# Sparse attention and a gated MLP in one kernel: the transfers of weight blocks get sort keys of their own

## The chip, the cores and the metric

The kernel runs on one core of a Trainium2 chip. Its engines work side by side, each through its own list of instructions in order: TensorE (PE) multiplies, VectorE (DVE), ScalarE (ACT) and GpSimd (POOL) do the rest, and SyncE (SP) issues all the transfers from memory. They wait for one another through semaphores. The metric is the device time of one execution in microseconds, the median of several runs.

## The reference

Eight batches of attention with 8 heads, 576 positions and 64 columns per head. The first four heads see a band of 32 positions, the others every 32nd position. Its output is the input of a gated MLP that mixes positions with a 576 x 576 matrix.

```python
scores = scale * np.matmul(q, k.transpose(0, 1, 3, 2))
scores = np.where(masks[None, :, :, :], scores, -1000000000.0)
attn = np.exp(scores - np.max(scores, axis=-1, keepdims=True))
attn = attn / (np.sum(attn, axis=-1, keepdims=True) + 1e-09)
x = np.matmul(attn, v)                    # heads side by side: B, S, 512

h = np.maximum(x @ w_in, 0.0)             # w_in: 512 x 1024
u, v = (h[..., :512], h[..., 512:])
v_n = (v - mu) / np.sqrt(var + 1e-06)     # mean and variance over the 512 columns
v_s = np.einsum('ts,bsd->btd', w_spatial, v_n) + b_spatial[None, :, None]
return ((u * v_s) @ w_out).astype(np.float32)   # w_out: 512 x 512
```

## The kernel before

**Work.** Attention is done for pairs of heads, numbered `t` = 4 b + hp for batch b: two pairs with the band (`local_attention`) and two with the stride (`strided_attention`) in each batch. Scores go into PSUM (L460 and L603), DVE and ACT make the softmax (maximum or mask, exponential L517, sums, L422), DVE transposes the weights in blocks (L541, L657), ACT, POOL and DVE copy the pieces into `ptl` or `pts` (L370, L368), and TensorE multiplies them with the values (L570, L673). The result x^T is split into a rounded part and a remainder (ACT L390, DVE L378), because every large product is done as three products of rounded float32 parts.

The MLP of a batch has these steps: `moe_1` multiplies the v half (L870: 4 tiles of 128 positions, each 4 blocks of 3 matmuls with 512 columns) and normalises it in `chain` (ACT L828, DVE L833 to L841, POOL's power L846, DVE L853), then the u half (L912, 288 columns). `moe_tail` does the 64 last positions of one or two batches. `moe_2` multiplies with the spatial matrix (L993, and L1005 and L1006 for the tail rows), gates with u (DVE L1015), and multiplies with `w_out` (L1035); ACT takes the output out of PSUM (L390).

**Weights.** `weights` brings 12 blocks of 128 rows: of `w_in` the u half and the v half of four row blocks (here u0 to u3 and v0 to v3) and four of `w_out` (o0 to o3). They come as 64-bit numbers of 512 KB a block, and `weight` turns each into two float32 parts: ACT scales the upper words (L746), POOL or DVE takes the low bits (L754, L751), DVE merges (L762), then one engine rounds (L368 on ACT, L370 elsewhere) and DVE subtracts the remainder (L378). The first four blocks in the order of their conversion land in one buffer (`vn_0`), the others in turn in `u` and `g` buffers, so a later one waits until an earlier one is converted. `spatial_weights` brings the four blocks of the spatial matrix (`x_0` and `x_1`, each with two) and its tail (`x_2`).

**Order.** Nothing runs in the order in which it is written. Every operation is added with a key, the engines that can do it, and costs; `Program.order` plays the program through with these costs, lets every engine take the smallest key among the operations that are ready, and the instructions are written out in the order and on the engines that came out. `KEYS` holds numbers that set the order: `a` for the attention of `t` = 0 to 7, `v`, `u`, `o`, `s` and `t` for the weight blocks, `fill` for the clearing of buffers, `lead` for later attention, `dp`, `dpt` and `near` for rules of choice. A transfer is an operation of SP with a key too: for a weight block it was the key of the conversion less 25 (in `weight` and `spatial_weights`). Fillers (L1168) are matmuls that keep TensorE busy at the start. SP's list is a queue as well: a transfer whose buffer isn't free holds up all those behind it.

Of the kernel before, what the change touches and what calls it, by code (L numbers as in the profile page):

```python
# [11 lines left out]
I32 = mybir.dt.int32  # L12
# [25 lines left out]
TAIL = S - 4 * P  # L38
NT = 4
KEYS = {  # L40
    "a": (-1127.3, -1221.6, -672.3, -526.1, 101.7, 33.0, 113.1, 239.5,),
    "v": (-238.9, -1399.6, -76.4, -73.7,),
    "u": (-43.5, -131.3, -12.3, -34.7,),
    "s": (684.8, 251.9, 2902.8, 2024.9,),
    "t": (1654.0,),
    "o": (6.6, -58.9, 103.7, 587.0,),
    "cst": (-1558.0,),
    "lead": (-1.36,),
    "fill": (50.5, 1235.4, -3578.4, 1164.7, -177.7, 809.5,),
    "dp": (849, -9544,),  # L50
    "dpt": (181.75,),
    "near": (198.57,),
}
WARM_END, WARM_GAP, WARM_COST, WARM_COLS, WARM_SHARE = 110000.0, 700.0, 427.0, 256, 0.8
PE_MASKED, APART = (0, 1, 2, 3), (0, 1)
# [254 lines left out]
def attention_moe(ctx, tc, qT, kT, vl, vs, cst, eye, w_in, w_out, wsp, wtail, out):  # L310
# [85 lines left out]
    def load(key, dst, src, writes, nbytes, reads=()):  # L396
        add(key, [(DMA, nbytes / DMA_RATE)], lambda eng: eng.dma_start(dst(), src), reads, writes)
# [323 lines left out]
    def x_tok(t):  # L721
        return [(xs[t], i, c0) for i in range(2) for c0 in ((0, 3) if t % NHP < 2 else (0, 1))]

    def weight(key, src, n, dst, tok, stage):

        buf, i = stage
        if src.dtype == F32:
            val = lambda: buf().bitcast(F32).rearrange(FLAT[len(buf.ring.shape)])[:, 2 * i * n : 2 * i * n + n]
            load(key - 25, val, src, [(buf, i, 0), (buf, i, 1)], P * n * 4)
        else:
            raw = lambda dt: buf().bitcast(F32).rearrange(FLAT[len(buf.ring.shape)])[
                :, 2 * i * n : 2 * (i + 1) * n
            ].bitcast(dt)
            half = lambda j, dt=I32: raw(dt).rearrange("p (n t) -> p n t", t=2)[:, :, j]
            low, top = (buf, i, 0), (buf, i, 1)  # L740
            val = lambda dt=F32: half(1, dt)
            load(key - 25, lambda: raw(I32), src.bitcast(I32), [low, top], P * n * 8)

            add(
                key, [(ACT, 110 + 0.87 * n)],
                lambda eng: eng.activation(val(), val(), AF.Prelu, scale=2.0**-112, alpha=2.0**32),  # L746
                [], [top],
            )
            def lowest(eng):
                if hasattr(eng, "bn_stats"):  # L750
                    eng.tensor_scalar(half(0), half(0), 29, None, op0=ALU.logical_shift_right)  # L751
                else:
                    byte = raw(U8).rearrange("p (n t) -> p n t", t=8)[:, :, 3]
                    eng.tensor_scalar(half(0), byte, 1 / 32, -15.5 / 32, op0=ALU.mult, op1=ALU.add)  # L754
# [5 lines left out]
            add(  # L760
                key, [(DVE, 70 + 1.04 * n)],
                lambda eng: eng.scalar_tensor_tensor(  # L762
                    half(1), half(1), 3, half(0),
                    op0=ALU.logical_shift_left, op1=ALU.bitwise_or,
                ),
                [low], [top], port=(DVE,),
            )
# [26 lines left out]

    def spatial_weights():
        for i in range(NT):
            key = KEYS["s"][i]
# [451 lines left out]
```

## Time and profile before

| | |
|---|---|
| median of 3 runs | 526.38 us (526.30 to 526.54) |
| the profiled execution | 526.95 us, its span 524.8 us, mean clock of TensorE 0.993 |
| start of the last matmuls (L1035) and of ACT's last copy | 515.0 us and 521.5 us |
| VectorE's longest full stretch | 20 to 80 us |
| weight blocks | 12 x 512 KB, and 6 x 288 KB for the spatial matrix |

The span is the time from the first to the last instruction of the profiled execution. A row of the engines' list in order of time gives the start in us, the duration in us, the engine, the line of the code, the operation, what it writes and reads, and how many in a row; in brackets the idle time before it and what ended it. In a group of the page the numbers behind the bar are the busy time in us and the mean of one in ns, then the engine's idle time before them. TensorE's clock is given as a share of its full speed.

### The profile page before, as it was taken

To read this page: it belongs to the slowest core of one execution; us is meant where nothing else is said; L and a number is where in the kernel's file an instruction comes from. 1 tells how busy PE (TensorE), PEld (TensorE's weight loads), DVE (VectorE), ACT (ScalarE), POOL (GpSimd) and SP (SyncE) were. 2 spreads that over 40 slices of the span, in tenths; PEclk is the share of its full clock that TensorE was granted. 3 is DMA by queue.
4 is the path that set the end of the run, shared out by engine and by line. 5 is a ranking of instruction groups with operands and counts; after the bars stand their busy time and mean duration, and the time that the engine had idled before them with its cause. 6 is when DMAs were issued, how large, how long until landed. Compare 5 with 4: busy or idle time off the path is not lost.

```text
span 524.8 us, 14567 instructions
## 1 busy us (share of the span) xinstructions
PE 509.3 (97%) x5982; PEld 467.8 (89%) x5982; DVE 327.1 (62%) x1019; ACT 238.1 (45%) x738; POOL 87.9 (17%) x170
## 2 busy tenths in 40 slices
PE   6798999999999999999999999999999999999997
PEld 3567799888998899989999899998999899998997
DVE  3999998684754848558556767757557652426132
ACT  6677956655653665126532365324543243213111
POOL 2364423120210212002110120102101020001000
PEclk9799999999999999999999999999999999999999
DMA  7779353622233213142222222332021200110011
GB/s 247 263 263 347 133 195 103 188 92 88 66 134 125 87 58 117 55 134 78 79 103 78 85 78 80 132 116 70 3 78 64 87 1 1 46 45 1 1 45 47
DMA packets 26242, 52.65 MB, mean 100 GB/s; under 512 B 3136, under 2 KB 11584, under 8 KB 26176
## 3 DMA queue, kind: packets, MB, share of 16 engines
q1 hardware_dynamic: 26176, 51.72, 30.0%
q8 instruction: 47, 0.77, 0.6%
q14 instruction: 19, 0.16, 0.1%
HBM read 42.27 MB, written 9.44 MB: 99 GB/s over the span
## 4 chain that ended last, share of the span: by engine, by line
PE 85%; DVE 6%; DMA 2%; POOL 2%; issue 2%; ACT 2%; SPq 0%; POOLq 0%; DVEq 0%; ACTq 0%
PE m L1035 20%; PE m L993 17%; PE m L912 17%; PE m L870 17%; PE po L673 3%; PE po L570 3%; PE s L460 2%; PE s L603 2%; PE m L1005 2%; PE m L1006 2%; DMA k<-kT 1%; DMA kbd<-kT 1%; POOL bn L846 1%; POOL ptl L370 1%; DVE bn L833 1%
## 5 line engine op out<-in xcount | busy, mean ns | idle before, releaser
L993 PE MATMUL m<-wsp_sb,vn 128*128 128x288 f32 x768 | 111.5, 296 | 1.0 <-DVE wsp_sb L378 1.0
L1035 PE MATMUL m<-g,w_out_sb 128*128 128x288 f32 x768 | 107.6, 298 | 0.3 <-DVE g L378 0.3
L912 PE MATMUL m<-x,w_in_sb 128*128 128x288 f32 x768 | 105.5, 297 | 1.8 <-ACT vv L828 1.1
L993 PEld LDWEIGHTS m<-wsp_sb,vn 128*128 128x128 f32 x768 | 105.1, 189 | 2.1 <-DVE wsp_sb L378 1.3
L912 PEld LDWEIGHTS m<-x,w_in_sb 128*128 128x128 f32 x768 | 103.3, 188 | 3.4 <-ACT vv L828 1.3
L1035 PEld LDWEIGHTS m<-g,w_out_sb 128*128 128x128 f32 x768 | 103.5, 188 | 1.1 <-DVE g L378 0.5
L870 PE MATMUL m<-w_in_sb,x 128*128 128x512 f32 (+1 forms) x408 | 99.1, 398 | 0.1
L870 PEld LDWEIGHTS m<-w_in_sb,x 128*128 128x128 f32 (+1 forms) x408 | 74.2, 185 | 19.6 <-DVE w_in_sb L378 0.4
L390 ACT COPY o<-m 128x288 f32<-128x288 f32 x60 | 23.7, 399 | 94.8 <-PE m L1035 88.5
L846 POOL TENSOR_TENSOR bn<-bn,sel 128x1 f32<-128x1 f32 (+1 forms) x37 | 22.3, 604 | 201.4 <-DVE bn L841 178.6
L1015 DVE TENSOR_TENSOR u<-m,u 128x288 f32<-128x288 f32 x64 | 28.2, 454 | 41.1 <-PE m L1006 40.7
L370 POOL TENSOR_SCALAR ptl<-pc 32x320 f32<-32x320 f32 (+3 forms) x77 | 30.3, 394 | 125.0 <-DVE pc L541 50.9
L517 ACT ACTIVATE pl<-pl,ml 128x64 f32<-128x64 f32 (+1 forms) x140 | 46.8, 337 | 3.4 <-DVE ml L497 3.4
L828 ACT ACTIVATE vv<-m 128x512 f32<-128x512 f32 (+1 forms) x37 | 22.1, 597 | 48.8 <-PE m L870 47.4
L378 DVE TENSOR_TENSOR x<-po,x 128x288 fp32r<-128x288 f32 x64 | 27.5, 447 | 25.0 <-ACT x L390 24.5
L926 ACT ACTIVATE u<-m 128x288 f32<-128x288 f32 x64 | 25.7, 409 | 36.7 <-PE m L912 36.2
L833 DVE BATCH_NORM_STATS2 bn<-vv 128x6 f32<-128x512 f32 (+1 forms) x37 | 25.5, 689 | 25.0 <-ACT vv L828 24.6
L853 DVE TENSOR_SCALAR vv<-vv,bn 128x512 f32<-128x512 f32 (+1 forms) x37 | 20.5, 556 | 17.1 <-POOL bn L846 17.0
L378 DVE TENSOR_TENSOR g<-u,g 128x288 fp32r<-128x288 f32 x64 | 28.3, 456 | 3.4 <-ACT g L368 2.1
L390 ACT CAST x<-po 128x288 fp32r<-128x288 f32 x53 | 20.4, 399 | 17.2 <-PE po L570 10.5
L392 DVE CAST x<-po 128x288 fp32r<-128x288 f32 x11 | 4.9, 453 | 36.7 <-PE po L673 28.3
L368 ACT COPY ptl<-pc 32x320 f32<-32x320 f32 (+3 forms) x69 | 24.4, 354 | 5.3 <-DVE pc L541 4.0
(118 smaller groups left out, 588.7 us busy)
## 6 DMA issues: line engine op xcount, KB each, us to landing
q<-qT SPq DMA_DIRECT2D x32, 295.0 KB, 4.2
outT<-o SPq DMA_DIRECT2D x64, 144.0 KB, 1.8
v_raw<-vs SPq DMA_DIRECT2D x15, 512.0 KB, 3.6
v_raw<-vl SPq DMA_DIRECT2D x16, 384.0 KB, 4.2
k<-kT SPq DMA_DIRECT2D x16, 304.0 KB, 4.6
kbd<-kT SPq DMA_DIRECT2D x32, 144.0 KB, 3.9
vn<-w_in SPq DMA_DIRECT2D x4, 512.0 KB, 5.5
u<-w_in SPq DMA_DIRECT2D x3, 512.0 KB, 6.5
```

The lines of the kernel that those rows point to most:

```text
L370: eng.tensor_scalar(dst(), src(), 1.0, 0.0, op0=ALU.mult, op1=ALU.add)
L378: eng.tensor_tensor(dst(), src(), f32(hi()), op=ALU.subtract)
L390: eng.copy(dst(), src())
L517: eng.activation(p_sb()[:m, u, :], src, AF.Exp, bias=st()[:m, u : u + 1], scale=SCALE if masked else -1.0, **total,)
L833: lambda eng: eng.bn_stats(bn()[:m, 0:6], v()[:m]), [(v,)], [(bn,)],
L846: lambda eng: eng.tensor_tensor(bn()[:m, 9:10], bn()[:m, 8:9], sel[:m, 0:1], op=ALU.pow),
L870: eng.matmul(v_ps()[:m, :], x_at(kt)[:, a, :], w_in_sb[:, w, kt, HF:], start=(n == 0 and i == 0), stop=(n == NT - 1 and i == 2),)
L912: eng.matmul(u_ps()[:, :HS], w_in_sb[:, w, kt, f * P : (f + 1) * P], xs[NHP * b + kt]()[:, a, r], start=(n == 0 and i == 0), stop=(n == NT ...
L926: lambda eng, u=u, f=f, u_ps=u_ps: eng.activation(u()[:, f * HS : (f + 1) * HS], u_ps()[:, :HS], AF.Relu),
L993: eng.matmul(s_ps()[:, :HS], vn()[:, a, kt, fs], wsp_sb[:, w, kt, r], start=(kt == 0 and i == 0), stop=False,)
L1015: lambda eng, ug=ug, s_ps=s_ps: eng.tensor_tensor(ug(), s_ps()[:, :HS], ug(), op=ALU.mult),
L1035: eng.matmul(o_ps()[:, :HS], w_out_sb[:, w, f, e * P : (e + 1) * P], g[a]()[:, f, :], start=(f == 0 and i == 0), stop=(f == NT - 1 and i = ...
```

## The change

The transfers of all weight blocks get keys of their own (`lv`, `lu`, `lo`, `ls`), where they had the key of the conversion less 25. All other numbers of `KEYS` are new too. The operations are the same; what changes is their order, the choice among engines and which buffer a block lands in. The new file has four lines more, so its line numbers are 4 higher from there on (L766 for L762).

```diff
 KEYS = {
-    "v": (-238.9, -1399.6, -76.4, -73.7,),
-    "u": (-43.5, -131.3, -12.3, -34.7,),
+    "v": (-216.6, -1140.4, -156.0, 19.8,),
+    "u": (-158.4, -165.3, 0.3, 367.0,),
...
+    "lv": (-430.1, -2526.4, -200.5, -140.6,),
+    "lu": (-99.7, -488.1, -137.6, -250.6,),
+    "lo": (435.1, 82.8, -874.1, 81.6,),
+    "ls": (781.6, 39.6, 3113.7, 831.6, 1021.7,),
...
-    def weight(key, src, n, dst, tok, stage):
+    def weight(key, fetch, src, n, dst, tok, stage):
...
-            load(key - 25, val, src, [(buf, i, 0), (buf, i, 1)], P * n * 4)
+            load(fetch, val, src, [(buf, i, 0), (buf, i, 1)], P * n * 4)
...
-            load(key - 25, lambda: raw(I32), src.bitcast(I32), [low, top], P * n * 8)
+            load(fetch, lambda: raw(I32), src.bitcast(I32), [low, top], P * n * 8)
...
                 jobs.append((
-                    KEYS[name][i], w_in[rows, cols], HF,
+                    KEYS[name][i], KEYS["l" + name][i], w_in[rows, cols], HF,
...
-                KEYS["o"][i], w_out[rows, :], DM, lambda j, i=i: w_out_sb[:, j, i], ("w_out", i),
+                KEYS["o"][i], KEYS["lo"][i], w_out[rows, :], DM, lambda j, i=i: w_out_sb[:, j, i], ("w_out", i),
...
-            load(key - 25, src, wsp[i * P : (i + 1) * P, :], [half], P * S * 4)
+            load(KEYS["ls"][i], src, wsp[i * P : (i + 1) * P, :], [half], P * S * 4)
...
-            load(key - 25, lambda i=i: raw(i), wtail[i], [halves[i]], P * S * 4)
+            load(KEYS["ls"][NT], lambda i=i: raw(i), wtail[i], [halves[i]], P * S * 4)
```

**First place: transfers after the start.** SP's queue from the 17th row on, before. `vn_0` holds v2 here, `u_0` v3, `g_0` o1, `u_1` u0, `g_1` u3 and `u_2` u2.

```order
L397 DMA vn_0_93<-w_in 128x1024
L397 DMA u_0_427<-w_in 128x1024
L397 DMA g_0_449<-w_out 128x1024
L397 DMA u_1_477<-w_in 128x1024
L397 DMA g_1_496<-w_in 128x1024
L397 DMA q_4_531<-qT 128x590
L397 DMA k_2_540<-kT 128x608
L397 DMA u_2_551<-w_in 128x1024
```

The same place now. `u_0` is v2, `g_1` v3, `u_1` u2, `vn_0` u0, `u_2` u3, and `x_0` is block 1 of the spatial matrix.

```order
L401 DMA u_0_402<-w_in 128x1024
L401 DMA g_1_428<-w_in 128x1024
L401 DMA u_1_450<-w_in 128x1024
L401 DMA vn_0_93<-w_in 128x1024
L401 DMA q_4_496<-qT 128x590
L401 DMA k_2_511<-kT 128x608
L401 DMA v_raw_3_534<-vl 128x768
L401 DMA u_2_547<-w_in 128x1024
L401 DMA x_0_332<-wsp 128x576
```

The `w_out` block has left this place (it comes six rows later, in `g_0`), u2 has moved ahead of u0, and u3, which stood among the five, now takes the buffer that v2 leaves.

**Second place: conversion on VectorE.** VectorE's rows from about 38 us on, before; between the last row of `x_6` and these stand a merge (of `u_1`) and the remainder of o1.

```order
L762 SCALAR_TENSOR_TENSOR g_1_496<-g_1_496 128x512
L378 TENSOR_TENSOR w_in_sb_62<-u_1_477,w_in_sb_62 128x512
L833 BN_STATS bn_0_578<-vv_0_571 128x6
L378 TENSOR_TENSOR w_in_sb_62<-g_1_496,w_in_sb_62 128x512
L837 BN_AGGR bn_0_578<-bn_0_578 128x2
L833 BN_STATS bn_1_594<-vv_1_582 128x6
L841 TENSOR_SCALAR bn_0_578<-bn_0_578 128x1
L762 SCALAR_TENSOR_TENSOR u_2_551<-u_2_551 128x512
L837 BN_AGGR bn_1_594<-bn_1_594 128x2
L853 TENSOR_SCALAR vv_0_571<-vv_0_571,bn_0_578 128x512
L841 TENSOR_SCALAR bn_1_594<-bn_1_594 128x1
L378 TENSOR_TENSOR w_in_sb_62<-u_2_551,w_in_sb_62 128x512
```

And now; only a merge (L766, of `vn_0`) stands between `x_6` and these.

```order
L382 TENSOR_TENSOR w_in_sb_62<-u_1_450,w_in_sb_62 128x512
L382 TENSOR_TENSOR w_in_sb_62<-vn_0_93,w_in_sb_62 128x512
L837 BN_STATS bn_0_575<-vv_0_568 128x6
L837 BN_STATS bn_1_586<-vv_1_577 128x6
L841 BN_AGGR bn_0_575<-bn_0_575 128x2
L841 BN_AGGR bn_1_586<-bn_1_586 128x2
L845 TENSOR_SCALAR bn_0_575<-bn_0_575 128x1
L845 TENSOR_SCALAR bn_1_586<-bn_1_586 128x1
L766 SCALAR_TENSOR_TENSOR u_2_547<-u_2_547 128x512
L857 TENSOR_SCALAR vv_0_568<-vv_0_568,bn_0_575 128x512
L382 TENSOR_TENSOR wsp_sb_64<-x_0_332,wsp_sb_64 128x576
L382 TENSOR_TENSOR w_in_sb_62<-u_2_547,w_in_sb_62 128x512
```

The last remainder of `w_in` is u2's (`u_2`) before and u3's (`u_2`) now, and a spatial block has come ahead of it. On TensorE the blocks of L912 follow this order: `m_8` and `m_9` take `x_3` and `x_4` and then, past an L460, `x_5` and `x_6` before; now `x_3` to `x_5`, then `x_6`, then the L460.

**Third place: ahead of the first L1035.** VectorE before, at the products with the gate (`u_4`):

```order
L417 RECIPROCAL ml0_78<-ml0_78 128x10
L422 TENSOR_TENSOR pl0_76<-pl0_76,ml0_78 128x640
L378 TENSOR_TENSOR tail_0_996<-vv_4_929,tail_0_996 64x512
L541 STREAM_TRANSPOSE pc_5_1019<-pl0_76 128x640
L378 TENSOR_TENSOR x_7_1028<-po_8_1012,x_7_1028 128x288
L370 TENSOR_SCALAR ptl_73<-pc_5_1019 32x8x32
L378 TENSOR_TENSOR x_7_1028<-po_9_1021,x_7_1028 128x288
L370 TENSOR_SCALAR ptl_73<-pc_5_1019 32x2x32
L1015 TENSOR_TENSOR u_4_712<-m_17_917,u_4_712 128x288
L1015 TENSOR_TENSOR u_4_712<-m_18_933,u_4_712 128x288
L1015 TENSOR_TENSOR u_4_712<-m_19_947,u_4_712 128x288
L1015 TENSOR_TENSOR u_4_712<-m_20_957,u_4_712 128x288
```

And now (the two masks are the last of `t` = 5, whose softmax is in `pl0`):

```order
L382 TENSOR_TENSOR tail_0_992<-vv_4_895,tail_0_992 64x512
L501 ISA pl0_76,ml0_78<-s_4_921,cst_sb_61 64x64
L501 ISA ml0_78 64x1
L501 ISA pl0_76,ml0_78<-s_5_923,cst_sb_61 64x64
L501 ISA ml0_78 64x1
L1019 TENSOR_TENSOR u_4_682<-m_17_865,u_4_682 128x288
L1019 TENSOR_TENSOR u_4_682<-m_18_879,u_4_682 128x288
L1019 TENSOR_TENSOR u_4_682<-m_19_890,u_4_682 128x288
L417 TENSOR_SCALAR ml0_78<-ml0_78 128x10
L1019 TENSOR_TENSOR u_4_682<-m_20_1007,u_4_682 128x288
L382 TENSOR_TENSOR g_5_1079<-u_4_682,g_4_1040 128x288 x4
L421 RECIPROCAL ml0_78<-ml0_78 128x10
```

The product, the transpose and the copies of `t` = 5 have moved behind the gate. On TensorE the L570 of `t` = 5 (`po_10`, `po_11`) moves with them: before, it stood directly ahead of the first L1035, now it comes after the whole group of 48.

More of the change, by code (lines that the diff above doesn't have):

```diff
@@ L40 @@
 KEYS = {
-    "a": (-1127.3, -1221.6, -672.3, -526.1, 101.7, 33.0, 113.1, 239.5,),
-    "v": (-238.9, -1399.6, -76.4, -73.7,),
-    "u": (-43.5, -131.3, -12.3, -34.7,),
[L44 to L52, printed above, removed]
+    "a": (-825.9, -1662.1, -696.1, -506.6, 76.7, 35.0, 162.7, 122.5,),
+    "v": (-216.6, -1140.4, -156.0, 19.8,),
+    "u": (-158.4, -165.3, 0.3, 367.0,),
+    "s": (2476.0, -453.8, 2782.5, 3198.4,),
+    "t": (2534.3,),
+    "o": (641.4, -137.9, 1268.2, 1486.2,),
+    "cst": (-2628.8,),
+    "lead": (-0.22,),
+    "fill": (170.7, 2011.8, -4312.7, 693.0, -265.9, 735.5,),
+    "dp": (844, -15182,),
+    "dpt": (83.09,),
+    "lv": (-430.1, -2526.4, -200.5, -140.6,),
+    "lu": (-99.7, -488.1, -137.6, -250.6,),
+    "lo": (435.1, 82.8, -874.1, 81.6,),
+    "ls": (781.6, 39.6, 3113.7, 831.6, 1021.7,),
+    "near": (122.22,),
 }
```

## The prediction

> **What bounds the kernel now.** I read the page first, then busy time by stretches of the span, then TensorE's own rows with the waits printed behind them.
>
> ```profile
> span 524.8 us, 14567 instructions
> PE 509.3 (97%) x5982; PEld 467.8 (89%) x5982; DVE 327.1 (62%) x1019; ACT 238.1 (45%) x738; POOL 87.9 (17%) x170
> ```
>
> ```profile
> 10.00:20.00 10.00, 4.35 (x143) 2.90 (x144) 7.26 (x21) 6.37 (x26) 1.88 (x5) 0.66 0.89 296
> 20.00:40.00 20.00, 19.10 (x233) 13.98 (x231) 19.57 (x39) 15.61 (x33) 10.96 (x16) 1.00 0.72 246
> 40.00:74.00 34.00, 30.91 (x489) 27.40 (x488) 31.44 (x100) 26.28 (x85) 15.21 (x24) 1.00 0.61 213
> 74.00:150.00 76.00, 75.94 (x1019) 70.28 (x1019) 52.55 (x199) 43.49 (x154) 14.45 (x30) 1.00 0.39 123
> ```
>
> The columns are stretch, PE, PEld, DVE, ACT, POOL, clock, DMA share, GB/s. TensorE is short of work in three places only: before 20 us (while the first keys arrive), a little until 40, and 3.09 us between 40 and 74. After that it is full, apart from the 3.4 us after its last matmul. In 40 to 74 VectorE is busy 92% and in 20 to 40 98%: weight conversion and the first attention share it. An order of work can therefore gain there and nowhere else.
>
> ```profile
> 39.85 1.76 PE L912 MATMUL m<-x,w_in_sb 128*128 128x288 f32 x12
> 42.78 0.54 PE L912 MATMUL m<-x,w_in_sb 128*128 128x288 f32 x2 [0.27 <-ACT w_in_sb L368]
> 43.76 1.60 PE L912 MATMUL m<-x,w_in_sb 128*128 128x288 f32 x10 [0.44 <-DVE w_in_sb L378]
> 46.47 9.92 PE L912 MATMUL m<-x,w_in_sb 128*128 128x288 f32 x72 [1.11 <-ACT vv L828]
> 64.17 3.69 PE L993 MATMUL m<-wsp_sb,vn 128*128 128x288 f32 x26 [1.02 <-DVE wsp_sb L378]
> 73.58 1.61 PE L1035 MATMUL m<-g,w_out_sb 128*128 128x288 f32 x10 [0.25 <-DVE g L378]
> ```
>
> These five waits are the whole 3.09 us. Counted from start to start they cost more, since the pipe refills. The prices of undisturbed work:
>
> ```profile
> 112.56 1.14 PE po L570 x24
> 126.94 0.90 PE s L460 x58
> 469.74 11.21 PE m L870 x48
> 480.94 12.80 PE m L912 x96
> ```
>
> So a 288-column matmul takes 12.80/96 = 0.133 us and a 512-column one 0.2335. From 39.85, 12 matmuls and one L460 end at 39.85 + 1.60 + 0.90 = 42.35; the next starts at 42.78 (0.4 lost). Two more are done at 43.05, and the next starts at 43.76 (0.7). Ten end at 45.09; 46.47 is 1.4 late. The same sum gives 1.3 at 64.17 and 0.5 at 73.58: **4.3 us in all** is what the changed order can win in this stretch.
>
> **Until 39.85 nothing moves that TensorE waits for.** The first 16 rows of SP's queue are the same (two `vn_0` transfers swap places). One clearing, of `pp1`, goes from ACT to DVE ahead of that of `kbd`, and one filler matmul goes.
>
> ```profile
> 10.19 1.19 SPq L397 DMA_DIRECT2D kbd<-kT  x2
> ```
>
> TensorE waits for keys there, and `kbd` is filled only from 10.19 on, long after either clearing: I cost this at nothing. Without that cover it would be 0.5 us. On DVE, ACT and POOL the rows up to `x_6` are the old ones with other weights in them, one for one, so `x_6` is complete at 36.6 and L870 ends at 39.85 as before.
>
> **Conversions.** A block of `w_in` takes a scaling (L746), low bits (L754), a merge (L762), a rounding (L368, L370) and a remainder (L378). u0 to u3 and v0 to v3 are the half blocks of `w_in`, o0 to o3 the blocks of `w_out`. Before, o1 stood among them; now all of `w_in` comes first, u2 early and u3 last.
>
> ```profile
> 34.20 1.13 DVE L762 SCALAR_TENSOR_TENSOR g<-g 128x512 int32<-128x512 int32 x1
> 35.86 0.81 DVE L378 TENSOR_TENSOR x<-po,x 128x288 fp32r<-128x288 f32 x2
> 36.54 0.64 POOL L754 TENSOR_SCALAR g<-g 128x512 int32<-128x512 uint8 x1
> 36.59 1.13 DVE L762 SCALAR_TENSOR_TENSOR u<-u 128x512 int32<-128x512 int32 x1
> 37.64 0.68 DVE L378 TENSOR_TENSOR w_out_sb<-g,w_out_sb 128x512 fp32r<-128x512 f32 x1
> 40.05 0.67 DVE L378 TENSOR_TENSOR w_in_sb<-g,w_in_sb 128x512 fp32r<-128x512 f32 x1
> 41.53 0.94 POOL L846 TENSOR_TENSOR bn<-bn,sel 128x1 f32<-128x1 f32 x1 [0.29 <-DVE bn L841]
> 42.50 0.55 DVE L853 TENSOR_SCALAR vv<-vv,bn 128x512 f32<-128x512 f32 x1 [0.36 <-POOL bn L846]
> 43.02 0.68 DVE L378 TENSOR_TENSOR w_in_sb<-u,w_in_sb 128x512 fp32r<-128x512 f32 x1
> ```
>
> ```profile
> L517 ACT ACTIVATE pl<-pl,ml 128x64 f32<-128x64 f32 (+1 forms) x140 | 46.8, 337 | 3.4 <-DVE ml L497 3.4
> L828 ACT ACTIVATE vv<-m 128x512 f32<-128x512 f32 (+1 forms) x37 | 22.1, 597 | 48.8 <-PE m L870 47.4
> L833 DVE BATCH_NORM_STATS2 bn<-vv 128x6 f32<-128x512 f32 (+1 forms) x37 | 25.5, 689 | 25.0 <-ACT vv L828 24.6
> L846 POOL TENSOR_TENSOR bn<-bn,sel 128x1 f32<-128x1 f32 (+1 forms) x37 | 22.3, 604 | 201.4 <-DVE bn L841 178.6
> ```
>
> Before, u3 (`g`) is done at 40.7 and u2 (`u`, the last row) at 43.7. DVE rows overlap by some 0.07, so a remainder or merge steps on by 0.6, an L853 by 0.46. In the new order DVE goes on from `x_6` at 36.6: merge of u0 1.05, remainders of u2 and u0 1.2, two L833 1.2, four small rows 0.3: 40.35. The merge of u3 0.6: 40.95. `vv_0` waits for POOL's power, 0.94 from 40.6: its L853 runs 41.6 to 42.1; `wsp_sb` of block 1 0.65, remainder of u3 0.65: **u2 is done at 38.2, but u3 only at 43.4.** If the merge of u0 takes 0.68, as alone (POOL's piece of 36.54 stands elsewhere now), and the power 0.60, its mean, it is 42.7. L912 has 18 matmuls until 39.85 + 2.4 = 42.25, then waits 0.5 to 1.2: I take **0.9**.
> The page "SBUF — State Buffer" of the Trainium skill ("SBUF: two separate sides") says that a DVE instruction with two SBUF inputs and a GpSimd one that reads SBUF exclude each other wholly. POOL ended at 37.18, and 37.18 + 0.54 is the 37.72 at which the merge ends, so the trace agrees; by it the merge steps by 0.6 and the gain is 0.4 more.
>
> The 6 matmuls with `x_6` and L460 (0.8 + 0.9) end at 45.0 to 45.2, `m_10` at 46.8. `m_11` takes the bank of `m_7`, freed by `vv_3`, which takes the buffer of `vv_1`. DVE from 43.4: remainder of `vv_0` 0.6, L853 of `vv_1` 0.5, `bn_2` 0.9 (it waits for `vv_2`), remainder of `vv_1` 0.6: 46.0. ACT is then in a scaling of 0.6, and the relu takes 0.6: 47.2. **0.45** lost; the old 1.11 at 46.47 was the same wait one tile earlier. L912 ends at 55.3, `m_16` (12 x 0.2335) at 58.1.
>
> **Spatial weights.** DVE from 46.0: six mask rows 1.0, `bn_3` 0.8, L853 of `vv_2` 0.45, four mask rows 0.8, then seven rows of 0.6 to 0.7 (merges of o1 and o2, remainders of `vv_2`, `vv_3`, o1 and o2, an L853) 4.45, two of them at the pace of ACT's L517: block 0 of `wsp` is done at 54.6, block 3 at 55.6, block 2, after the product and transpose of `t`=4 and the o0 block, at 61.6. TensorE does blocks 0 and 1 from 58.1 to 60.5, then L570 and L460 (1.14 + 0.90), which need `ptl`: POOL makes 5 pieces from 57.5, at 0.61 each as the 6 before.
>
> ```profile
> 58.26 3.64 POOL L370 TENSOR_SCALAR ptl<-pc 32x320 f32<-32x320 f32 x6 [2.70 <-DVE pc L541]
> 67.28 1.01 DVE L422 TENSOR_TENSOR pl<-pl,ml 128x640 f32<-128x640 f32 x1
> 69.04 0.85 DVE L541 STREAM_TRANSPOSE pc<-pl 128x640 f32<-128x640 f32 x1
> 71.61 1.55 DVE L1015 TENSOR_TENSOR u<-m,u 128x288 f32<-128x288 f32 x4
> ```
>
> That ends at 60.5 to 60.7: **0.2**. The second half of L993 starts at 62.8, after block 2, so the old 1.3 goes. The tail (`tail_0`) is the chain of `bn_4` from 61.7: L833 0.6, `x_7` and merge 1.8, power 1.1 beside them, L853 0.5, masks 0.9, remainder 0.65: 67.0, where TensorE asks at 66.4: **0.5**.
>
> **Gate.** The products into `u_4` (71.61 before) no longer stand behind the product, transpose and copies of `t`=5 (1.01 + 0.85 + 0.8) and start at about 67.6; four of them and a remainder later, at 69.9, L1035 can start, where TensorE is ready at 69.8: **0.2**. As a check: 73.45 before against 70.05, less one L570 of 1.14 that was done by then and now comes later, is 2.3. By the waits it is 4.3 - (0.9 + 0.45 + 0.2 + 0.5 + 0.2) = 2.05. I take **2.0**.
>
> **Later.** DVE must still do the postponed 2.7 us. It has room:
>
> ```profile
> 91.72 0.46 DVE L378 TENSOR_TENSOR g<-u,g 128x288 fp32r<-128x288 f32 x1 [0.65 <-ACT g L368]
> 95.57 0.22 DVE L497 CUSTOM_DVE_ANT_0 pl<-s,cst_sb 128x64 f32<-128x64 f32 x1 [3.40 <-PE s L460]
> ```
>
> L870 of batch 1 now does `x_7` to `x_9` first and `x_10` last; by summed rows `x_10` is ready at 103.5, and TensorE asks for it at 105.5. From 150 us on both programs do the same matmuls with small attention pieces a few places earlier or later, in a kernel that is full there: nothing.
>
> **The sum.** The profiled execution took 526.95 with a span of 524.8; less 2.0 is 524.95 for a run like it. The median of the three runs is 526.38, 0.57 lower, so I forecast **524.4**.
>
> **Rivals.**
> *u3's transfer is late, and the kernel is slower.* u3 goes into `u_2`, which waits until v2 has left `u_0` (34.3).
>
> ```profile
> 36.01 0.33 SPq L397 DMA_DIRECT2D u<-w_in  x1
> 40.07 1.17 POOL L754 TENSOR_SCALAR u<-u 128x512 int32<-128x512 uint8 x1 [2.89 <-DMA u<-w_in]
> g<-w_in SPq DMA_DIRECT2D x1, 512.0 KB, 10.3
> ```
>
> The old `u_2` took 4.0 us, sent alone; the old `g_1`, behind four others, 10.3. Sent at 34.4 the new one lands between 38.4 and 44.7. Its scaling, low bits and merge then fit until a landing of 39.5; each later us holds L912 and all of TensorE by one. From 41.5 the gain is gone; at 44.7 the kernel takes 526.4 + 3.2 = 529.6; half-way, 527.5. For it: five blocks of 512 KB, `q_4`, `k_2` and `v_raw_3`, 3.5 MB by the page, are asked for from 21.6 on, at 246 GB/s 14 us, so the queue empties near 35.8 and the transfer is not quite alone. Against: one block fewer is ahead than before. 1 in 10.
> *The gain is given back.* `x_10` or `x_9` comes late for batch 1, because attention 5 to 7 was pushed behind the gate; DVE would need 4 us more than summed. Then 526.4. 15 in 100.
> *The waits go altogether* (powers at 0.60, transfers early): 4.3 off, 522.1. 7 in 100.
> *The clock drops.*
>
> ```profile
> PE m L603 <- DMA kbd<-kT: 4.4, 1, 4.4
> ```
>
> It was 0.66 in 10 to 20 us, where TensorE waited 4.4 us in one piece, and 1.00 in all later stretches with waits up to 1.11; the new ones are no longer than 1.2, so this stays out, and only the first rival could bring it.
> The page "TensorE: Matmul & The Clock Gate" of the Trainium skill (Part 1) puts the threshold at an idle window of some 3.4 us; the rows agree, and by it no term changes.
>
> **Numbers.** Forecast 68 in 100, for 523.2 to 525.8. The range to hold 8 in 10 reaches down to where most of the waits are gone and up past the given-back gain: 522.6 to 526.8. A measurement of this kernel can tell about 0.2% (1.05 us) from no change, so faster is below 525.3: most of the forecast, and the third rival, 0.68; within 0.2%: the rest of the forecast and the second rival, 0.20; slower: the first rival and a little of the second, 0.12.
>
> **What would show it.** TensorE at 39.85 as before; one L912 wait near 42.3 for `w_in_sb`, under 1.3 us; no wait of L993 for `wsp_sb`; L1035 starting near 70; none for `x` near 105. It is wrong if POOL's low bits of `u_2` start after 40 (first rival), or if L870 of batch 1 waits.

## The result, and the profile after

The changed kernel takes **524.29 us** (median of 14 runs, 522.62 to 526.53), where the old one took 526.58 beside it (14 runs, 526.16 to 528.14): the ratio is 0.9949 (95% interval 0.9938 to 0.9961), 0.4 to 0.6% faster. A second set of runs of the same kernel, on another occasion, gave 0.9955 (0.9938 to 0.9971). The profiled execution took 523.65 us.

First the head of the page after, then busy time by stretches as before (stretch, PE, PEld, DVE, ACT, POOL, clock, DMA share, GB/s).

```profile
span 521.6 us, 14553 instructions
PE 508.8 (98%) x5980; PEld 468.1 (90%) x5980; DVE 332.9 (64%) x1042; ACT 229.1 (44%) x717; POOL 83.6 (16%) x168
```

```profile
10.00:20.00 10.00, 5.85 (x146) 3.37 (x148) 7.26 (x21) 6.37 (x26) 1.87 (x5) 0.55 0.86 269
20.00:40.00 20.00, 19.55 (x232) 14.82 (x233) 18.76 (x43) 15.94 (x33) 10.85 (x17) 0.97 0.82 275
40.00:74.00 34.00, 32.85 (x495) 30.41 (x494) 32.17 (x103) 26.52 (x85) 13.30 (x21) 1.00 0.65 216
74.00:150.00 76.00, 76.00 (x1109) 69.80 (x1108) 55.37 (x209) 39.82 (x149) 14.39 (x32) 1.00 0.37 117
```

Between 40 and 74 us TensorE is idle for 1.15 us instead of 3.09, and VectorE is fuller than before (95%). TensorE's rows there, with the waits behind them:

```profile
39.54 2.81 PE L916 MATMUL m<-x,w_in_sb 128*128 128x288 f32 x20
42.96 0.80 PE L916 MATMUL m<-x,w_in_sb 128*128 128x288 f32 x4 [0.61 <-DVE w_in_sb L382]
43.69 0.97 PE L464 MATMUL s<-k,q 64*32 64x64 f32 x72
44.59 9.86 PE L916 MATMUL m<-x,w_in_sb 128*128 128x288 f32 x72
61.56 3.82 PE L997 MATMUL m<-wsp_sb,vn 128*128 128x288 f32 x27
65.92 0.40 PE L1009 MATMUL m<-wt_h,tail 128*128 128x288 f32 x1 [0.54 <-DVE tail L382]
69.01 6.26 PE L1039 MATMUL m<-g,w_out_sb 128*128 128x288 f32 x45
```

Two waits are left: 0.61 for u3, 0.54 for the tail. L997 runs through without one, and L1039 starts right behind the scores before it, without a wait for the gate.

VectorE's three rows that set u3, and POOL's row before them:

```profile
36.27 0.68 DVE L766 SCALAR_TENSOR_TENSOR vn<-vn 128x512 int32<-128x512 int32 x1
41.09 0.55 DVE L857 TENSOR_SCALAR vv<-vv,bn 128x512 f32<-128x512 f32 x1 [0.45 <-POOL bn L850]
42.23 0.68 DVE L382 TENSOR_TENSOR w_in_sb<-u,w_in_sb 128x512 fp32r<-128x512 f32 x1
```

```profile
39.94 1.73 POOL L850 TENSOR_TENSOR bn<-bn,sel 128x1 f32<-128x1 f32 x2 [0.60 <-DVE bn L845]
```

Where the gain is made is read from three marks of each profile: the start of the u half (L912, L916), the start of the first group of the `w_out` products (L1035, L1039; the first batch's gate), and that of the second. The mark of the first gate is the start from which the group runs on without a stop; in the old kernel a single matmul of it stands ahead of that, at 72.92. The rows of the second and the last, of before and of after:

```profile
141.31 6.66 PE L1035 MATMUL m<-g,w_out_sb 128*128 128x288 f32 x48
514.85 6.56 PE L1035 MATMUL m<-g,w_out_sb 128*128 128x288 f32 x48
```

```profile
137.89 6.56 PE L1039 MATMUL m<-g,w_out_sb 128*128 128x288 f32 x48
511.67 6.56 PE L1039 MATMUL m<-g,w_out_sb 128*128 128x288 f32 x48
```

From L912 to the first gate the old kernel takes 73.58 - 39.85 = 33.73 us. They hold one L570 of 1.14 that the new one does later, and the gate's single matmul of 0.13, so it is 32.46 like for like; the new one takes 69.01 - 39.54 = 29.47: 3.0 less. From the first to the second gate it is 67.73 + 0.13 = 67.86 against 68.88 - 1.14 = 67.74, 0.1 less. From the second to the last it is 373.54 against 373.78, 0.24 more.

One correction of names: the product, transpose and copies near 57 us, which the prediction gives to `t` = 4, belong to pair 5, and those near 68 us, which the section on the change and the prediction give to `t` = 5, to pair 4. Pair 5 comes first in both kernels. Below they have their right names.

### The profile page after: what moved, and what is told of

Same layout as the page of the kernel before. It is cut to its first block, busy times and chain, and to the rows that moved or that the text cites. A ratio compares the mean times of both kernels' runs of the same rounds, so it can differ in the third digit from the quotient of the medians.

```text
span 521.6 us, 14553 instructions
## 1 busy us (share of the span) xinstructions
PE 508.8 (98%) x5980; PEld 468.1 (90%) x5980; DVE 332.9 (64%) x1042; ACT 229.1 (44%) x717; POOL 83.6 (16%) x168
## 4 chain that ended last, share of the span: by engine, by line
PE 88%; DVE 3%; DMA 3%; ACT 3%; SPq 1%; issue 1%; POOL 0%; ACTq 0%; DVEq 0%
PE m L1039 20%; PE m L997 18%; PE m L916 17%; PE m L874 17%; PE po L574 3%; PE po L677 3%; PE s L464 2%; PE s L607 2%; PE m L1009 2%; PE m L1010 2%; DMA g<-w_in 1%; DMA k<-kT 1%; DMA kbd<-kT 1%; PE po L1172 1%; ACT pl L521 1%; SPq L401 1%
## 5 line engine op out<-in xcount | busy, mean ns | idle before, releaser
L997 PE MATMUL m<-wsp_sb,vn 128*128 128x288 f32 x768 | 110.9, 295 | 0.0
L1039 PE MATMUL m<-g,w_out_sb 128*128 128x288 f32 x768 | 107.2, 297 | 0.0
L916 PE MATMUL m<-x,w_in_sb 128*128 128x288 f32 x768 | 106.1, 297 | 0.6 <-DVE w_in_sb L382 0.6
L997 PEld LDWEIGHTS m<-wsp_sb,vn 128*128 128x128 f32 x768 | 105.1, 189 | 0.9
L916 PEld LDWEIGHTS m<-x,w_in_sb 128*128 128x128 f32 x768 | 103.5, 188 | 2.3 <-DVE w_in_sb L382 0.8
L1039 PEld LDWEIGHTS m<-g,w_out_sb 128*128 128x128 f32 x768 | 103.5, 188 | 0.5
L874 PE MATMUL m<-w_in_sb,x 128*128 128x512 f32 (+1 forms) x408 | 99.9, 398 | 0.1
L874 PEld LDWEIGHTS m<-w_in_sb,x 128*128 128x128 f32 (+1 forms) x408 | 74.0, 185 | 19.5 <-DVE w_in_sb L382 0.4
L374 POOL TENSOR_SCALAR ptl<-pc 32x64 f32<-32x64 f32 (+3 forms) x74 | 28.8, 390 | 125.0 <-PE po L574 74.9
L521 ACT ACTIVATION_READ_ACCUMULATOR pl<-pl,ml 128x1 f32 (+1 forms) x140 | 26.5, 189 | 0.0
L501 DVE CUSTOM_DVE_ANT_0 pl<-s,cst_sb 128x64 f32<-128x64 f32 (+1 forms) x140 | 22.5, 214 | 3.1 <-PE s L464 3.1
```

The source lines that it names most:

```text
L374: eng.tensor_scalar(dst(), src(), 1.0, 0.0, op0=ALU.mult, op1=ALU.add)
L501: eng.tensor_tensor_reduce(out=p_sb()[:m, u, :], in0=s_ps[u % 2]()[:m, f0 : f0 + 2 * STRIDE], in1=msk[:m], scale=-SCALE, scalar=3.0e38, op ...
L521: eng.activation(p_sb()[:m, u, :], src, AF.Exp, bias=st()[:m, u : u + 1], scale=SCALE if masked else -1.0, **total,)
L874: eng.matmul(v_ps()[:m, :], x_at(kt)[:, a, :], w_in_sb[:, w, kt, HF:], start=(n == 0 and i == 0), stop=(n == NT - 1 and i == 2),)
L916: eng.matmul(u_ps()[:, :HS], w_in_sb[:, w, kt, f * P : (f + 1) * P], xs[NHP * b + kt]()[:, a, r], start=(n == 0 and i == 0), stop=(n == NT ...
L997: eng.matmul(s_ps()[:, :HS], vn()[:, a, kt, fs], wsp_sb[:, w, kt, r], start=(kt == 0 and i == 0), stop=False,)
```

## The experiments

A new number in `KEYS` makes the planner write a wholly new order, so it can't test one step. All kernels below but one therefore replay a list that was recorded from the planner, with single entries moved:

```diff
-        issued = self.order()
-        fillers = self.fillers(issued)
+        code = json.loads(zlib.decompress(base64.b85decode(ORDER)))
+        issued, fillers = [(0, n, (PE, DVE, ACT, POOL, DMA)[e]) for n, e in code], FILLERS
```

All compute the whole result. This table has the marks of every profile but those of the two hybrids that follow it (us; "keys" is the first start of L603 or L607, "u half" and "gate" as above) and the ratio of the time to that of the old kernel beside it.

| kernel | keys | u half | first gate | between | second gate | ratio (95%) |
|---|---|---|---|---|---|---|
| old | 16.61 | 39.85 | 73.58 | 33.73 | 141.31 | 1 |
| new | 15.42 | 39.54 | 69.01 | 29.47 | 137.89 | 0.9949 (0.9938 to 0.9961) |
| new again (e9) | 15.82 | 39.29 | 68.11 | 28.82 | 137.73 | 0.9955 (0.9938 to 0.9971) |
| e3, pair 4 ahead of the gate | 15.22 | 39.50 | 73.48 | 33.98 | 142.38 | 1.0019 (1.0002 to 1.0036) |
| e4, o1 early | 15.78 | 39.84 | 70.82 | 30.98 | 140.52 | 0.9986 (0.9973 to 0.9999) |
| e8, o1 fetched early | 18.01 | 42.22 | 71.64 | 29.42 | 141.22 | 0.9972 (0.9957 to 0.9986) |
| e12, old with o1 late | 14.63 | 39.77 | 73.57 | 33.80 | 141.41 | 1.0019 (1.0006 to 1.0031) |
| e5, u3 first | 15.44 | 39.62 | 68.90 | 29.28 | 138.30 | 0.9963 (0.9949 to 0.9977) |
| e7, tail first | 16.11 | 40.36 | 70.07 | 29.71 | 139.33 | 0.9955 (0.9939 to 0.9971) |
| e6, v2 fetched early | 17.06 | 41.05 | 71.03 | 29.98 | 139.97 | 0.9955 (0.9939 to 0.9970) |
| e10, keys fetched early | 13.66 | 39.47 | 69.37 | 29.90 | 138.87 | 0.9950 (0.9930 to 0.9970) |
| e11, all four of these | 15.28 | 39.69 | 69.02 | 29.33 | 138.28 | 0.9955 (0.9938 to 0.9972) |

The old kernel, e3 and e12 do the L570 (L574) of pair 4 ahead of the first gate, which is 1.14 of "between"; in the old kernel the single matmul of the gate is another 0.13.

**Where along the span (e1, e2).** Two hybrids were made: the new order up to 68 us of the plan and then the old one, and the reverse.

> The changed kernel's recorded order for everything that its planner begins before 68 us (on the chip some 75 us), and behind that the old kernel's order and engines. Theory (the whole gain is made between 40 and 74 us): L1039 starts near 69 us as in the changed kernel, and the time is that of the changed kernel, 524.3 us, 0.4% below the kernel before. Rival (the gain, or part of it, comes from the other order of the later batches): less than half of it, 525.4 us or more.

> The mirror of it: the old kernel's recorded order up to 68 us of its plan, and behind that the changed kernel's order and engines. Theory: L1035 starts near 73.5 us and the time is that of the kernel before, 526.4 us (ratio 1.000). Rival (later batches): 525.4 us or less. If the time is above 526.8 us the two halves don't fit together, and the later order costs something.

Their times are 530.11 us (ratio 1.0059, 1.0045 to 1.0072) and 534.62 (1.0146, 1.0131 to 1.0161), both slower than either kernel: the halves don't fit, as the second expectation allowed for. The longest waits at the seam, of the first and of the second hybrid:

```profile
PE po L677 <- DMA k<-kT: 3.0, 1, 3.0
```

```profile
PE po L673 <- issue: 5.3, 1, 5.3
```

So the times tell nothing of the question, but the stages do. The first hybrid comes to its gate like the new kernel, the second like the old one:

```profile
70.21 6.03 PE L1039 MATMUL m<-g,w_out_sb 128*128 128x288 f32 x43
```

```profile
73.60 1.59 PE L1035 MATMUL m<-g,w_out_sb 128*128 128x288 f32 x10 [0.27 <-DVE g L378]
```

From its second gate (145.34) to the end of its last matmul (525.59) the first hybrid, with the old order there, takes 380.25 us, the old kernel 380.10, the new one 380.34. The later batches gain nothing; the rival that the gain lies there falls.

**Pair 4 ahead of the gate (e3).**

```diff
+DVE  L417 L421 L426 L545 L374 x3   (pair 4)
 DVE  L1019 u_4 x4, L382 g x4       (the gate)
-DVE  L417 L421 L426 L545 L374 x3
+ACT  L372 ptl x4
 ACT  L372 g x4
-ACT  L372 ptl x4
+PE   L574 x2
 PE   L1039 x16
-PE   L574 x2
```

> The changed kernel with one thing put back: VectorE's sum, reciprocal, product, transposition and copies of attention pair 4 (L417 to L374), the copies of ACT, and TensorE's two L574 of that pair stand again ahead of the gate. VectorE has 2.9 us more ahead of the gate products (1.0 + 0.85 + 0.7 + 0.3). Theory (VectorE is full from 53 to 70 us, so what stands ahead of the gate sets when L1039 starts; one L574 of 1.14 us fills part of it): L1039 starts at 71.5 to 72.5 us and the time is 1.4 to 2.2 us above the changed kernel's, 525.7 to 526.5 us. Rival (this place costs 0.2 us only, as the prediction has it, and the waits before it make the gain): at most 0.5 us above, 524.8 us.

It is 0.6 to 0.7% slower than the new kernel (1.0019 against 0.9949 and 0.9955), about 3.5 us, which is more than the theory gave and more than the whole gain. VectorE's rows:

```profile
68.06 0.17 DVE L417 TENSOR_SCALAR ml<-ml 128x10 f32<-128x10 f32 x1 [1.37 <-ACT pl L521]
68.52 0.82 DVE L426 TENSOR_TENSOR pl<-pl,ml 128x640 f32<-128x640 f32 x1
69.38 0.84 DVE L545 STREAM_TRANSPOSE pc<-pl 128x640 f32<-128x640 f32 x1
70.26 1.16 DVE L374 TENSOR_SCALAR ptl<-pc 32x128 f32<-32x128 f32 x3
71.45 1.55 DVE L1019 TENSOR_TENSOR u<-m,u 128x288 f32<-128x288 f32 x4
```

and TensorE's:

```profile
71.90 1.65 PE L574 MATMUL po<-ptl,v_raw 128*64 128x96 f32 x24 [2.40 <-POOL ptl L374]
73.48 3.75 PE L1039 MATMUL m<-g,w_out_sb 128*128 128x288 f32 x18
```

The expectation counted VectorE's rows only. The sum waits another 1.37 us for ACT's exponentials of the same pair, and the gate stands behind it: all of a softmax chain, with two engines, comes ahead of the first product of the gate. The gate is back at 73.5, where the old kernel had it, although everything ahead of 66 us came within 0.5 us of the new kernel's times.

The gate's own matmuls are slower besides: 18 take 3.75 us, where 45 took 6.26 in the new kernel. The clock granted to TensorE (last but two of the columns) is half behind the wait of 2.40 us:

```profile
71.00:73.00 2.00, 1.10 (x20) 1.10 (x22) 1.97 (x6) 1.94 (x6) 1.24 (x4) 0.88 0.70 176
73.00:75.00 2.00, 2.00 (x14) 1.78 (x11) 1.97 (x7) 0.47 (x2) 0.00 (x0) 0.50 0.43 134
75.00:77.00 2.00, 2.00 (x14) 2.00 (x13) 1.90 (x5) 0.40 (x1) 0.00 (x0) 0.77 0.03 8
```

So this profile loses 73.48 - 69.01 - 1.14 = 3.3 us up to the gate, and another 1.2 from there to the second gate (68.90 against 67.74), which the old kernel, with its shorter waits, doesn't pay.

**o1 early in the new kernel (e4, e8) and late in the old one (e12).**

```diff
 SP   L401 g_1<-w_in (v3)
+SP   L401 g_0<-w_out (o1)
 SP   L401 u_1<-w_in (u2)
...
+DVE  L766 g_0   (o1; then x_6, L766 of u2)
+DVE  L382 w_out_sb<-g_0
 DVE  L766 vn_0  (u0)
 DVE  L382 w_in_sb<-u_1 (u2)
```

> The changed kernel with the block o1 of w_out fetched and converted among the blocks of w_in again (in the old kernel's pattern: its merge and remainder ahead of those of u0, its rounding on POOL). VectorE has 1.3 us more ahead of u3, and 1.3 us less later. Theory A (each wait is paid by itself, as the prediction's sum has it): the wait of L916 for u3 grows from 0.7 to about 1.9 us and the time by 1.2 us, to 525.5 us. Theory B (VectorE's backlog up to the gate is what counts, in whatever order): L916 waits 1.9 us, but the wait of 0.5 us before L1009 goes and the start of L1039 stays within 0.4 us of 69.0: 524.3 to 524.8 us.

It is 0.3 to 0.4% slower than the new kernel, 1.6 to 2.0 us. The rows of o1 on ACT and POOL move with these, and the rounding of u2 goes from POOL to ACT, as o1's takes its place; so it isn't VectorE's rows alone that changed. TensorE's rows:

```profile
43.29 0.53 PE L916 MATMUL m<-x,w_in_sb 128*128 128x288 f32 x2 [0.79 <-ACT w_in_sb L372]
44.32 0.81 PE L916 MATMUL m<-x,w_in_sb 128*128 128x288 f32 x4 [0.50 <-DVE w_in_sb L382]
70.82 5.36 PE L1039 MATMUL m<-g,w_out_sb 128*128 128x288 f32 x38
```

The two waits of the old kernel for `w_in_sb` are back, and "between" is 30.98, 1.0 above the longest of the kernels that leave this stretch alone (28.82 to 29.98) and 1.5 above most. VectorE's 1.3 us less later win nothing: theory A. The transfer alone:

> The changed kernel with only the transfer of o1 put back among those of w_in (ahead of u2's); its conversion stays late. It tells the transfer's part from the conversion's in the run before, which put both back and was 1.9 us slower than the changed kernel. Theory (VectorE's rows, not the transfers, were what o1 cost): u2, u0 and u3 land some 1.5 to 2 us later but are still in time, L916 starts at 39.5 to 40 and the time is within 0.5 us of the changed kernel's: ratio 0.994 to 0.996. Rival (the transfers set it): 1 to 2 us slower, ratio 0.997 or more, with a wait of ACT for u<-w_in or vn<-w_in near 30 to 35 us.

The ratio (0.9972) lies between the two, and its interval touches both; it is inside the rival's bound (0.997 or more). ACT does wait for u2's transfer, as the rival had it:

```profile
35.75 0.68 ACT L750 ACTIVATE u<-u 128x512 f32<-128x512 f32 x1 [1.12 <-DMA u<-w_in]
```

But TensorE pays nothing for it in this profile: L916 waits for no block of `w_in`, and "between" is 29.42. Its u half starts late, at 42.22, because the keys did (18.01), ahead of the transfer that was moved. That the conversion and not the transfer costs is thus read from the stage, not from the time; what makes the 0.2% of this run stays open.

For the last of these runs, in the old kernel, o1 took the places of o0, o0 those of o3, and o3 came last.

> The old kernel with one part of the change: the block o1 of w_out is fetched and converted late. o1 takes the places of o0 in all queues, o0 those of o3, and o3 is converted last (its merge behind the remainders of the spatial matrix, its remainder behind that of the tail). The mirror of the run that put o1 back. VectorE has 1.3 us less ahead of u2 and 1.3 us more ahead of the gate. Theory (each us that VectorE does less ahead of u2 is won there, and TensorE keeps it): the waits at 42.8, 43.8 and 46.5 us, together 2.5 us from start to start, shrink by 1.0 to 1.8; L993 waits for wsp_sb at 64 as before or less; L1035 waits some 0.5 us more for g or w_out_sb; the time falls by 0.6 to 1.3 us, ratio 0.9975 to 0.999. Rival (the work that is put off is only waited for later): L1035 starts at 73.5 us as before, with over 1 us of wait for w_out_sb or g, ratio 1.000. Third (this step alone makes the gain): ratio below 0.9965.

The rival was right: the gate starts at 73.57, no earlier than in the old kernel (73.58 behind its single matmul). TensorE's rows first, then VectorE's:

```profile
42.34 1.89 PE L912 MATMUL m<-x,w_in_sb 128*128 128x288 f32 x12
45.36 9.86 PE L912 MATMUL m<-x,w_in_sb 128*128 128x288 f32 x72 [1.14 <-ACT vv L828]
63.28 3.73 PE L993 MATMUL m<-wsp_sb,vn 128*128 128x288 f32 x26 [1.30 <-DVE wsp_sb L378]
73.57 2.71 PE L1035 MATMUL m<-g,w_out_sb 128*128 128x288 f32 x18
```

```profile
67.00 1.01 DVE L422 TENSOR_TENSOR pl<-pl,ml 128x640 f32<-128x640 f32 x1
68.04 0.68 DVE L378 TENSOR_TENSOR tail<-vv,tail 64x512 fp32r<-64x512 f32 x1
68.75 0.69 DVE L378 TENSOR_TENSOR w_out_sb<-g,w_out_sb 128x512 fp32r<-128x512 f32 x1
69.36 0.84 DVE L541 STREAM_TRANSPOSE pc<-pl 128x640 f32<-128x640 f32 x1
71.79 1.55 DVE L1015 TENSOR_TENSOR u<-m,u 128x288 f32<-128x288 f32 x4
```

Both waits for `w_in_sb` are gone, L912 does its last 72 at 45.36 instead of 46.47, and L993 goes on 0.9 us earlier than before. But the products of the gate come at 71.79 (71.61 before), behind pair 4 and the block that was put off, and all of it is given back. The remainder of o3 stands here ahead of pair 4's transpose, which starts 0.32 later than before (69.36 against 69.04); without it, by an estimate from these rows, it would start 0.3 earlier. So the run shows that VectorE's work that is put off up to the gate is waited for there, and not what pair 4 alone costs. That the time is even 0.2% above the old one's the profile doesn't show: its execution took 527.00 us, the old kernel's 526.95.

**The two waits that are left (e5, e7).** Remainder of u3 ahead of that of block 1; rows of VectorE around the tail:

```diff
 DVE  L857 vv_0
+DVE  L382 w_in_sb<-u_2 (u3)
 DVE  L382 wsp_sb<-x_0
-DVE  L382 w_in_sb<-u_2 (u3)
```

```diff
-DVE  L382 x_7 (both halves)
+DVE  L857 vv_4
 DVE  L382 w_out_sb<-g_3 (o3)
-DVE  L857 vv_4
 DVE  L501 (two pairs of mask rows)
+DVE  L382 tail_0
 DVE  L501 (three pairs), L1019 u_4, L382 g x4
+DVE  L382 x_7 (both halves)
```

> The changed kernel with two neighbours on VectorE exchanged: the remainder of u3 (L382, 0.68 us) now ahead of that of block 1 of the spatial matrix (0.75 us). Theory (each wait of TensorE is paid by itself and nothing behind it takes a gain back): L916 waits 0.0 to 0.1 us for w_in_sb instead of 0.61, L1039 starts 0.5 to 0.65 us earlier (68.4), and the time is 0.6 us (0.1%) below the changed kernel's: ratio to the kernel before 0.9935 to 0.9942. Rival (VectorE has no idle time from 53 to 65 us, so the tail comes no earlier and the wait before L1009 grows by what was won): L1009 waits 1.1 us, the start of L1039 and the time stay.

> The changed kernel with three rows of VectorE moved around the tail: both remainders of x_7 (0.42 and 0.44 us) behind the gate, the remainder of o3 behind the normalising L857 of the tail, and the remainder of the tail ahead of three pairs of mask rows. The tail is ready some 0.7 us earlier. Theory: L1009 no longer waits (0.54 before), L1039 starts at 68.3 to 68.6 and the time is 0.5 to 0.7 us below the changed kernel's: ratio 0.9933 to 0.9942. Rival (the postponed rows make the gate late): L1039 waits for g 0.3 us or more and nothing is won.

Neither wins anything that the runs show. In the first, the wait for u3 is gone, one for ACT has come, and that for the tail has grown:

```profile
39.62 3.38 PE L916 MATMUL m<-x,w_in_sb 128*128 128x288 f32 x24
44.16 9.87 PE L916 MATMUL m<-x,w_in_sb 128*128 128x288 f32 x72 [0.27 <-ACT vv L832]
65.82 0.40 PE L1009 MATMUL m<-wt_h,tail 128*128 128x288 f32 x1 [0.84 <-DVE tail L382]
```

The gate comes 29.28 us behind the u half, 0.2 less than in the new kernel. In the second, the wait for the tail is down to 0.18, but "between" is 29.71. The unedited kernel itself tells why 0.6 us can't be seen here: taken again (e9), it has no wait for u3 at all and 0.38 for the tail,

```profile
39.29 3.69 PE L916 MATMUL m<-x,w_in_sb 128*128 128x288 f32 x24
64.98 0.40 PE L1009 MATMUL m<-wt_h,tail 128*128 128x288 f32 x1 [0.38 <-DVE tail L382]
68.11 6.66 PE L1039 MATMUL m<-g,w_out_sb 128*128 128x288 f32 x48
```

because POOL's two powers took 1.23 us together instead of 1.73:

```profile
39.67 1.23 POOL L850 TENSOR_TENSOR bn<-bn,sel 128x1 f32<-128x1 f32 x2 [0.52 <-DVE bn L845]
```

**The spread of the runs (e6, e9, e10, e11).** The new kernel's first 14 runs spread over 3.9 us. Moved in SP's queue were v2 ahead of `v_raw_2` (e6), and the first two `kbd` ahead of `q_2` (e10); e11 has both and the edits of e5 and e7.

```diff
+SP   L401 kbd<-kT x2
 SP   L401 q_2<-qT
-SP   L401 kbd<-kT x2
...
+SP   L401 u_0<-w_in (v2)
 SP   L401 v_raw_2<-vs
-SP   L401 u_0<-w_in (v2)
```

> The changed kernel with one row of SP's queue moved: the transfer of v2 (into u_0) ahead of that of v_raw_2, which waits for its buffer until 21.8 us and holds up all behind it. In the trace of the changed kernel ACT scales v2 at 27.89, right behind its other work; in the profile of the first hybrid it waits for that transfer until 29.14, and TensorE loses 0.9 us between 28 and 40. Theory (the landing of v2, which varies from one execution to the next, is what spreads the runs of the changed kernel over 3.9 us): ACT no longer waits for u<-w_in before 28 us, L916 starts at 39.2 to 39.5, the runs spread over less than 2 us and their median is 0.3 to 1 us below the changed kernel's: ratio 0.993 to 0.9945. Rival (the spread comes from the arrival of the first keys before 20 us, which this doesn't touch): spread and median as before, 0.995.

> The changed kernel itself, unedited, beside the next two on one chip. In the profiles so far of kernels with its first 40 us, L607 starts between 15.2 and 18.0 us with the landing of kbd, and L916 between 39.5 and 42.2. Theory (the landing of the first strided keys spreads the runs): ratio near 0.995 again, runs spread over 3 us or more.

> The changed kernel with the first two transfers of kbd moved ahead of that of q_2 in SP's queue; q_2 waits until 9.4 us for its buffer (freed by the first L464) and holds kbd up. Theory: they are sent at 5.3 to 6.5 us, L607 then waits for q_2 or kbd until 13 to 14.5 us and no longer as late as 18, the four fillers (L1172, 3.6 us at half the clock) are done before their successor's pieces are, L574 starts at 18.6 to 19.2 in every run; L916 can't start before some 39.5, since v2 still lands at 27.3 to 29. Runs spread over less than 2 us; median 0.3 to 1 us below that of the unedited kernel on the same chip. Rival (the early transfers only take bandwidth from k of pair 0, and the chain from there is what counts): L464 of pair 0 starts later than 11.5 us, no gain.

> The changed kernel with four edits: the first kbd transfers ahead of q_2, v2's transfer ahead of v_raw_2's, u3's remainder ahead of that of block 1 of the spatial matrix, and the tail's rows as in the run on the tail. Theory: L916 starts at 38.0 to 39.0 us, L1039 29.0 to 29.3 us behind it (29.47 in the changed kernel), and the time is 1 to 2 us below that of the unedited kernel on the same chip: ratio to the kernel before 0.991 to 0.993. Rival (what is won in front is waited for again at the next stage, as in the runs on u3 and on the tail): less than 0.5 us.

In e6 the rival holds: median 0.9955, and a spread of 3.1 us in eight runs. Its profile, of the longest of the eight executions (525.73 us), is late from one row on, the keys of the first strided pair:

```profile
17.06 1.19 PE L607 MATMUL m<-kbd,q 128*32 128x36 f32 x64 [4.73 <-DMA kbd<-kT]
```

In profiles of kernels with one and the same queue up to there, that row stands between 15.22 (e3) and 18.01 (e8), and where it is late all behind it is: from it to the u half it is 24.1 to 24.3 us in the new kernel, e3, e4, e5, e7 and e8 (25.05 in e1, where v2 landed late; 23.5 in e9). With `kbd` sent early (e10) L607 starts at 13.66, but its last rows wait for 16.04, and the u half starts at 39.47:

```profile
13.66 1.08 PE L607 MATMUL m<-kbd,q 128*32 128x36 f32 x57 [1.55 <-DMA q<-qT]
16.04 0.29 PE L607 MATMUL m<-kbd,q 128*32 128x36 f32 x4 [1.30 <-issue]
```

All four edits together give 0.9955, the same as the unedited kernel on that occasion. The spread of e10 and e11 is 2.6 and 2.3 us in six runs, that of the control 1.65, so the expectations on the spread (under 2 us for e10, 3 or more for the control) both missed; the runs are too few to tell a spread. The median of e10 is 0.5 us below the control's (523.81 against 524.34), well inside the intervals. That the landing of the keys spreads the runs is therefore supported by the profiles' marks, not shown by an edit. No version is clearly faster than the new kernel.

One test was left out: the new conversions with transfers tied to them again (key less 25). By the recorded lists, such a program would wait for itself: a transfer of pair 8 stands ahead of u3's and waits for L464 of pair 5, which stands on TensorE behind the L916 that needs u3. So the part of the transfers' own keys is argued only: no run shows that this order of conversions can't be had without them.

## Why the prediction was right

The forecast was 524.4 us, the median 524.29, and the gain was made where it was forecast, by the order of work between 40 and 74 us. That the number came so near is in part luck: the gain in that stretch was taken too small, and the runs traced show more than the medians.

- **Up to 39.85.** "Nothing moves that TensorE waits for": 39.54 and 39.29 in the two profiles of the new kernel. But the mark isn't fixed; with the keys late it stood at 42.22 (e8).
- **u3.** Forecast done at 43.4, or 42.7 with POOL's piece out of the way; it was done at 42.91. The merge of u0 took 0.68 with no POOL row beside it, so what "SBUF — State Buffer" of the Trainium skill ("SBUF: two separate sides") says of the exclusion agrees with the trace again; the merge of u2 at 33.89, beside a POOL row of 33.50 to 34.48, took 1.13. The wait, forecast at 0.9, cost 42.96 - (39.54 + 20 x 0.133) = 0.76, and nothing in the second profile. The price depended on the power on POOL, as the prediction said.
- **`vv` 0.45 and `ptl` 0.2.** Neither came in the new kernel. The first appears in two kernels without the wait for u3 (0.27 in e5, 0.75 in e11), but not in e9, which has no such wait either.
- **Spatial weights and tail.** No wait of L997, as forecast. The tail: 0.5 forecast, 0.54 and 0.38 measured.
- **Gate.** No wait, 0.2 forecast. L1039 at 69.01 and 68.11, forecast 70.0.
- **The size of the gain in this stretch** was the term that was mis-sized: 2.0 forecast, 3.0 by the first profile (like for like 32.46 against 29.47), 3.6 by the second. The new waits were forecast at 2.25 together and were 0.76 + 0.76 from start to start in the first; 4.3 less these is 2.8, near what it shows.
- **"From 150 us on ... nothing", and batch 1 at no cost.** No L874 of batch 1 waited for `x`, so the second rival didn't come. But between the first and the second gate the new kernel takes 0.1 us less (first profile) or 0.6 more (second: 137.73 - 68.11 - 1.14 = 68.48 against 67.86) than the old one, and behind it 0.2 more in both. What costs these isn't traced.
- **The profiles and the medians.** The last group of products starts 3.2 and 3.35 us earlier than in the old kernel (514.85 - 511.67 and 514.85 - 511.50), but the medians are only 2.3 apart. The traced execution of the old kernel took 526.95, 0.37 above its median; those of the new one took 523.65 and 523.32, 0.64 and 1.02 below theirs. The forecast subtracted its 2.0 from a median and couldn't know of this.
- **First rival.** u3's transfer was sent at 34.04 (34.4 forecast) and POOL had its low bits at 38.69, before the 39.5 up to which it costs nothing. The clock was 1.00 between 40 and 150 us in both profiles.

The method, adding up single waits, came out right for this order, but the runs show where it isn't safe. It priced the gate at 0.3 (0.5 before, 0.2 now), and counted the gain at the steps ahead of it. e12 makes a gain ahead of the gate (both waits for `w_in_sb` gone) and has lost all of it at 73.57; e3 has everything ahead of the gate as in the new kernel, within 0.5 us, and has lost all of it at 73.48. In both, as in the old kernel, pair 4 stands ahead of the gate, and in e12 VectorE has as much to do ahead of it as before, only later. Whether pair 4 alone would hold TensorE until 73.5 is not shown. With pair 4 behind the gate the earlier steps count (e4: o1 early then costs 1.0 to 1.5 us at the gate). The prediction's cross-check, the two starts of L1035 compared, had this in it, the list of waits had not.

## What to carry to other kernels

When waits are to be removed from a stage, look first for the place where its engines meet (here the gate) and work out when that place is ready with each thing in its way; a wait ahead of it is worth nothing while another chain holds the meeting place (e3), or when the work taken out of its way comes back ahead of the meeting place (e12). To test one step of a scheduler's order, record the order and move single entries, since a changed key changes everything. And take the unedited kernel's profile twice before believing a gain of half a us.

## What the runs showed of the hardware

The same queue of transfers delivered the first strided keys so that their matmuls started between 15.22 and 18.01 us. In the latest of these profiles (e8) issuing itself was slow; two of the key transfers held SP's queue for 4.36 us:

```profile
13.24 4.36 SPq L401 DMA_DIRECT2D kbd<-kT  x2
```

In the new kernel's first profile the same row has 2.42 us. And two small powers on POOL took 1.73 us in one execution and 1.23 in another, in the same place of the program.

Behind one wait of 2.40 us TensorE's granted clock was 0.50 from 73 to 75 us (e3), and the first gate's matmuls took 0.21 us apiece instead of 0.14 (3.75 / 18 against 6.26 / 45). Waits up to 1.40 us (e12) left it at 1.00 there. The threshold of some 3.4 us that stands in the prediction is longer than this wait: the measurement decides, and why so short a wait was enough isn't shown.
